# Recurrent outputs with tokens on partitions: scores and queries become the stationary operands, and reversed rows are shifted by DMA

## Chip, cores and metric

The kernel runs on one core of one Trainium2 chip. Times are device microseconds of one execution; the time of a kernel is the median of its runs. The engines are named as the profile names them: PE (matrix products), PEld (its weight loads), DVE (vector), ACT (scalar), POOL (GpSimd) and SP, whose queue issues all DMAs here.

## The reference

For 4 batches, 8 heads, 768 tokens and 40 features a head, a gated recurrence runs over the tokens; its output is laid out as rows of 320 features, mixed by a two-dimensional Fourier transform, normalised and passed through a two-layer network.

```python
for t in range(S):
    m_new = np.maximum(f_gate[:, :, t] + m, i_gate[:, :, t])
    f_stab = np.exp(f_gate[:, :, t] + m - m_new)
    i_stab = np.exp(i_gate[:, :, t] - m_new)
    C = f_stab * C + i_stab * outer(vt, kt)         # 40 x 40 a head
    n = f_stab * n + i_stab * kt
    h = C @ qt;  denom = np.maximum(np.abs(n . qt), 1.0)
    y[:, :, t] = sigmoid(o_gate[:, :, t]) * h / denom
x = y as (B, S, 320)
u = x + real(fft(fft(x, axis=1), axis=2))
un = (u - mean(u)) / sqrt(var(u) + 1e-6)
out = u + relu(un @ w_ch1) @ w_ch2                  # 320 -> 1280 -> 320
```

## The kernel before

**Tiles.** A chunk is 128 tokens, six to a batch. In batches 2 to 4 (numbered 1 to 3 in the code) a chunk is worked as two halves of 64 tokens, each with its own step of the state, and the 8 heads lie as two groups of four pairs (hip 0 and 1, pair p). Products on PE use a quarter of the array each (64 rows by 64 columns), and four of them, in the order TILES, run side by side. All values are fp32. What belongs to one chunk:

- `mlstm_load`, `mlstm_load_max`, `mlstm_load_decay` and `mlstm_load_o` fetch queries and keys (`qk`, features on partitions), keys and values with a column of ones (`kvt`, tokens on partitions), the running maxima (`W<-M_d`), the decays (`Gb<-G_d`) and the output gate (`so`). M_d and G_d are scratch in DRAM, written once in batch 1.
- `mlstm_exp` on ACT and `mlstm_mask` on POOL (L487) make the weights W of a pair of tokens; `halves_scores` makes the scores on PE, and `halves_weigh` on DVE (L643) multiplies them into W.
- `halves_to_state` makes the chunk's part of the next state on PE; `halves_decay` (POOL, L629) and `halves_add` (DVE, L638) build the state. Three state buffers rotate.
- `halves_from_state` multiplies the state (stationary) with the decayed queries qg (moving); `halves_from_chunk` multiplies the values (stationary) with W (moving), in two turns so that each turn's row groups write separate PSUM banks. A tiny ACT copy, `halves_between` (L670), stands between the turns. All small products are issued by the helper at L491. The result, `ph`, has features on partitions.
- `halves_gather` copies `ph` to SBUF on ACT (L568 to L579, with `mlstm_heads`), `halves_turn` transposes it on PE with four products against the identity (L681) so that tokens lie on partitions, and `mlstm_finish` on DVE (L696 to L703) divides by the denominator, applies the gate and writes rows of x. L703 is its last instruction and the last reader of the PSUM banks `heads`, in which both `ph` and the transposed copy lie.

**Order of tokens.** The Fourier part folds chunk c with chunk 5 - c, so chunks 2, 4 and 5 (BACKWARDS) hold their tokens in reverse and shifted by one; first tokens of chunks 0, 1 and 2 change places. `mlstm_heads` does this in its ACT copies; `h_first` is a small buffer on POOL for the swapped token.

**Order of work.** Every step is put into a plan by `at(slot, phase, function)`, and the plan is run in order of slot and phase (EVAC, FILL, MAIN, FILL_PE, that is 0 to 3). Engines execute their own instructions strictly in that order and wait for each other by semaphores. The network of one batch gives a slot its length (a block of products), and the recurrence of a later batch is filled in between: the recurrence of code batch 1 stands in slots 32 to 52, that of 2 from slot 50, that of 3 from 82, three slots a chunk. In `plan_halves`, with s the chunk's first slot, scores come at s, from_state and from_chunk at s+3, the copy at s+4, the transposes at slots s0 + (7, 10, 13, 16, 19, 19), the finish one slot after them.

Lines that also appear: L1013, L1022, L1084 and L1089 are products of the network's first layer, L1147 and L1203 of the second; L379 to L399 convert weights from float64 bits on DVE and ACT; L858 to L901 are products of the Fourier part, L944 its transposes; `mix_fold` (L778 to L797) adds and subtracts the chunk pairs of x, on DVE and partly POOL. L331 and L332 are transposes of weights that `halves_of_chunks` makes once for batches 2 to 4, and L335 and L336 their copies to SBUF.

Of the kernel before, what the change touches and what calls it, by code (L numbers as in the profile page):

```python
# [42 lines left out]
ORDER = (0, 5, 1, 4, 2, 3)  # L43
M_INIT = -1.0e30
# [8 lines left out]
def kernel(  # L53
# [87 lines left out]
    def gates(gp):  # L141
# [161 lines left out]

        def maxima_out():
            nc.sync.dma_start(out=M_d.rearrange("c i p t -> p c i t"), in_=M[0:BH].rearrange("p c (i t) -> p c i t", i=2))

        def halves_of_chunks(step):
# [8 lines left out]
            elif step == 1:  # L316
# [3 lines left out]
                nc.sync.dma_start(out=G_d[:, H:].rearrange("c p t -> p c t"), in_=g[H:BH])  # L320
            elif step == 2:
                d2 = late["dec2"] = free[0:BH, 3 * S:3 * S + BH // 2 * NS].rearrange("p (n c) -> p n c", c=NS)
                ends = g[0:BH].rearrange("p c (i t) -> p (c i) t", i=2)[:, :, LH - 1]
                nc.gpsimd.tensor_tensor(out=d2, in0=ends.unsqueeze(1).to_broadcast([BH, BH // 2, NS]),
                                        in1=spread_sb[:, L:].unsqueeze(2).to_broadcast([BH, BH // 2, NS]), op=OP.mult)
            elif step == 3:
                p2 = ps_h.tile([L, NT * BH + BH // 2 * NS], FP, name="p2", tag="ph")
                pt, pd = p2[:, 0:NT * BH], p2[:, NT * BH:]
                late["p2"] = [t.rearrange("p (n c) -> p n c", c=n) for t, n in ((pt, BH), (pd, NS))]
                for c in range(NT):  # L330
                    nc.tensor.transpose(late["p2"][0][:, c, :], wk[:, c, :], ident[0:BH, 0:BH])  # L331
                nc.tensor.matmul(late["p2"][1], spread_sb[:, 0:L], late["dec2"], start=True, stop=True)  # L332
            else:
                pt, pd = late["p2"]
                nc.vector.tensor_copy(out=colT[:, :, 1, H:], in_=pt[:, :, H:])  # L335
                nc.vector.tensor_copy(out=decB[:, NP:], in_=pd[:, NP:])  # L336

        at(12, FILL + 0.7, maxima_out)
        at(1, FILL + 0.2, parts, last)
# [9 lines left out]
        for n, (s, phase) in enumerate(((16, FILL + 0.2), (18, FILL + 0.3), (19, FILL + 0.4), (21, FILL_PE + 0.5),  # L349
                                        (26, FILL + 0.8))):  # L350
            at(s, phase, halves_of_chunks, n)
# [132 lines left out]
    def mlstm_mask(b, c):  # L484
        for i in range(2):
            W = chunks[b, c].W[i * LH:(i + 1) * LH]
            nc.gpsimd.affine_select(out=W, in_=W, compare_op=OP.is_ge, fill=0.0, base=0, pattern=[[0, H], [1, LH]],  # L487
                                    channel_multiplier=-1)
# [70 lines left out]
    def mlstm_heads(b, c, ph, parts=False):  # L559
# [3 lines left out]
        if b > 0:  # L563
            hT, before = (t.rearrange("p (hip m) t -> p hip m t", hip=2) for t in (hT, before))
        every, first, later = (tuple([slice(None)] * (len(ph.shape) - 1) + [t]) for t in
                               (slice(0, L), slice(0, 1), slice(1, L)))
# [27 lines left out]
    def side(n):  # L594
        return banks["heads"].rearrange("p hip (s m t) -> p s hip m t", s=2, t=L)[:, n]

    TILES = ((0, 0), (1, 1), (0, 1), (1, 0))

    def columns(c, n):

        return LH if c == 0 else n

    def halves_scores(b, c):
# [5 lines left out]
        for p in range(NP):  # L609
            for hip, i in TILES:  # L610
                r, t = slice(hip * 64, hip * 64 + D), slice(i * LH, (i + 1) * LH)
                product(k.ps[t, hip, p, :], k.qk[r, 1, p, t], k.qk[r, 0, p, t], True)

    def halves_to_state(b, c):
        k = chunks[b, c]
        for p in range(NP):
            for i, hip in TILES:
                if 2 * c + i < NS - 1:
                    r, h, n = slice(i * LH, (i + 1) * LH), hip * NP + p, columns(c, D)
                    product(k.pc[hip * 64:hip * 64 + n, i, p, :], k.k[r, h * D:h * D + n], k.vw[r, h, :], True)  # L620
# [11 lines left out]
    def halves_add(b, c, i):  # L632

        k, n = chunks[b, c], 2 * c + i
        if n == 0:
            nc.vector.tensor_copy(out=halves_state(k, 1), in_=k.pc[:, 0])
        elif n < NS - 1:
            nc.vector.tensor_tensor(out=halves_state(k, i + 1), in0=halves_state(k, i + 1), in1=k.pc[:, i], op=OP.add)  # L638
# [6 lines left out]
    def halves_from_state(b, c):  # L645

        k = chunks[b, c]
        k.ph = side(0)
        for m in range(2):
            for i in range(2):  # L650
                for hip, e in TILES:
                    if 2 * c + i > 0:
                        r, t, p = slice(hip * 64, hip * 64 + D), slice(i * LH, (i + 1) * LH), 2 * m + e
                        product(k.ph[e * 64:(e + 1) * 64, hip, m, t], k.C[i][r, p * D1:p * D1 + LH], k.qg[r, p, t],
                                m == 0 and i == (c == 0))

    def halves_from_chunk(b, c, turn):
# [4 lines left out]
        for m in range(2):  # L662
            for i, e in TILES:
                hip, n = i ^ turn, columns(c, D1)
                r, h = slice(i * LH, (i + 1) * LH), hip * NP + 2 * m + e
                product(k.ph[e * 64:e * 64 + n, hip, m, r], k.v[r, h * D1:h * D1 + n], k.W[r, h, :], False)

    def halves_between(b, c):

        nc.scalar.copy(out=warm[0:1, 0:1], in_=chunks[b, c].ph[0:1, 1, 1, L - 1:L])  # L670

    def halves_gather(b, c):
        k = chunks[b, c]
        k.hT = hT_bufs[(b * NT + c) % 2]
        mlstm_heads(b, c, k.ph)

    def halves_turn(b, c):
        k = chunks[b, c]
        px = side(0 if c == NT - 1 else 1)
        for p in range(NP):  # L680
            nc.tensor.transpose(px[:, p // 2, p % 2], k.hT[:, p, :], ident)  # L681
        k.px = px

    def mlstm_finish(b, c):

        k = chunks.pop((b, c))
        if c == 0:
            xs[b] = x_bufs[b % 2]
        px = k.px.rearrange("p (a pr) t -> p a pr t", a=2) if b == 0 else k.px
        h1 = px.rearrange("p a pr (two e) -> p a (pr two) e", two=2)  # L690
# [11 lines left out]
        x, sc = (t.rearrange("p (a h d) -> p a h d", a=2, d=D) for t in (xs[b][:, c, 0:DM], k.so))  # L702
        nc.vector.tensor_tensor(out=x, in0=h1[:, :, :, 0:D], in1=sc, op=OP.mult)  # L703

# [21 lines left out]
    def plan_halves(b, s0, stride=3):  # L726
        for c in range(NT):
            s = s0 + stride * c
            end = c == NT - 1
# [16 lines left out]
            at(s + 3, MAIN - 0.1 if end else FILL_PE, halves_from_state, b, c)  # L746
            at(s + 3, MAIN - 0.1 if end else FILL_PE, halves_from_chunk, b, c, 0)
            at(s + 3, MAIN if end else FILL_PE + 0.5, halves_between, b, c)
            at(s + 3, FILL_PE + 3, halves_from_chunk, b, c, 1)
            at(s + 4, FILL - 0.6, halves_gather, b, c)  # L750
            at(s + 4, FILL + 0.35, mlstm_tanh, b, c)
            t = s0 + (7, 10, 13, 16, 19, 19)[c]
            at(t, FILL_PE + 0.5, halves_turn, b, c)
            at(t + 1, MAIN + 0.55, mlstm_finish, b, c)
# [545 lines left out]
    plan_batch(2, 50, 83, s_mlp + 2 * MLP_SLOTS)  # L1300
    plan_batch(3, 82, 115, s_mlp + 3 * MLP_SLOTS)
# [102 lines left out]
def _layout(q, k, v, o_gate):  # L1404
# [4 lines left out]
    def token_major(t):  # L1409
        return t.reshape(B, H, NT, L, D).transpose(0, 2, 3, 1, 4)  # L1410

    qkT = np.stack([feature_major(q), feature_major(k)], axis=4)
# [3 lines left out]
    o = o_gate.transpose(0, 2, 1, 3).reshape(B, S, DM)[:, _tokens()]  # L1416
# [29 lines left out]
```

## Time and profile before

| | us |
|---|---|
| runs, median (lowest to highest) | 408.74 (404.95 to 409.12), 3 runs |
| profiled execution, its own time | 410.02 |
| its span, first to last instruction | 408.3 |
| busy: PE, PEld, DVE, ACT, POOL | 390.9, 285.3, 281.3, 182.1, 129.1 |

The chip's granted PE clock averages 0.99 of full speed in the profile. The recurrence of batches 2 to 4 lies between 62 and 284 us; from about 300 us on only the last batch's Fourier part and network remain. In a line of instructions the numbers are start and duration in us (timeline), or busy us, mean ns of one and idle time before them with what ended it (groups). A line of waits has who waited for whom, us in total, times, and the longest.

### The profile page before, as it was taken

What the parts mean: (1) busy time and instruction counts of PE and PEld (TensorE: products, weight loads), DVE (VectorE), ACT (ScalarE), POOL (GpSimd) and SP (SyncE); (2) the same over time, 40 slices, a digit from 0 to 9 for tenths busy, and PEclk for the clock granted to TensorE, in tenths of its full rate; (3) what the DMA queues carried; (4) which work ended last, traced back from release to release, by engine and by line L of the source; (5) the groups of instructions that cost most, each with busy time, mean ns of one, the idle gap of its engine ahead of it and who ended that gap; (6) DMA issues with size and microseconds to landing.
All of it is one profiled execution on the core that took longest, in us unless ns stands there. A gap on an engine that the chain in (4) does not pass through costs nothing.

```text
span 408.3 us, 10669 instructions
## 1 busy us (share of the span) xinstructions
PE 390.9 (96%) x4246; PEld 285.3 (70%) x4246; DVE 281.3 (69%) x669; ACT 182.1 (45%) x510; POOL 129.1 (32%) x228
## 2 busy tenths in 40 slices
PE   8999999999979999998999999998999999999996
PEld 6877555556547677765559998855569997556996
DVE  8789986798846539675874579966764786335652
ACT  6987258577640232555464315553450122455000
POOL 5555314477940641240074233440230000020000
PEclk9999999989999999999999999999999999999999
DMA  7989499487643352375001444300000000000000
GB/s 217 289 229 309 114 232 270 157 240 216 166 119 109 113 136 86 99 206 161 0 10 36 139 122 151 108 4 2 0 2 6 28 33 34 0 0 2 32 34 32
DMA packets 23836, 43.29 MB, mean 106 GB/s; under 512 B 5076, under 2 KB 12972, under 8 KB 23660
## 3 DMA queue, kind: packets, MB, share of 16 engines
q1 hardware_dynamic: 23788, 42.63, 35.8%
q8 instruction: 33, 0.54, 0.6%
q14 instruction: 15, 0.12, 0.1%
HBM read 38.49 MB, written 4.12 MB: 104 GB/s over the span
## 4 chain that ended last, share of the span: by engine, by line
PE 80%; DVE 12%; issue 3%; ACT 3%; POOL 1%; POOLq 0%; DVEq 0%; ACTq 0%
PE po L1203 17%; PE pm L1084 16%; PE po L1147 8%; PE pm L1089 5%; PE pm L1022 5%; PE ph L491 4%; PE ps L491 3%; PE pu L901 3%; PE pz L870 2%; PE ph L681 2%; PE put L944 1%; DVE stats L928 1%; PE pm L1013 1%; PE pz L858 1%; PE ph L532 1%
## 5 line engine op out<-in xcount | busy, mean ns | idle before, releaser
L1153 DVE SCALAR_TENSOR_TENSOR x<-po,rstd,x 128x160 f32<-128x160 f32 (+1 forms) x69 | 26.9, 394 | 38.0 <-PE po L1203 35.3
L1093 DVE TENSOR_TENSOR h<-h,pm 128x384 f32<-128x384 f32 x60 | 30.7, 550 | 31.2 <-PE pm L1084 17.2
L1084 PE MATMUL pm<-uT,w_sb 128*128 128x384 f32 x90 | 37.3, 501 | 0.2 <-DVE uT L1072 0.2
L464 ACT ACTIVATE W<-W,colT 128x64 f32<-128x64 f32 x144 | 37.4, 340 | 0.0
L1147 PE MATMUL po<-w_sb,h 128*128 128x320 f32 x120 | 36.1, 451 | 0.0
L629 POOL TENSOR_TENSOR C<-C,decB 128x164 f32<-128x164 f32 x30 | 17.3, 577 | 55.8 <-DVE C L638 45.5
L487 POOL TENSOR_SCALAR_AFFINE_SELECT W<-W 64x512 f32<-64x512 f32 x36 | 28.3, 785 | 17.2 <-ACT W L464 16.1
L1022 PE MATMUL pm<-uT,w_sb 128*128 128x384 f32 x80 | 31.4, 521 | 0.6 <-issue 0.4
L1147 PEld LDWEIGHTS po<-w_sb,h 128*128 128x128 f32 x120 | 23.0, 196 | 10.0 <-issue 1.6
L1203 PE MATMUL po<-T,S 128*128 128x160 f32 x180 | 28.0, 302 | 0.2 <-DVE x L1153 0.2
L474 POOL TENSOR_TENSOR qg<-qk,Gb 128x512 f32<-128x512 f32 (+1 forms) x21 | 27.2, 1297 | 1.1 <-DMA Gb<-G_d 1.1
L1203 PEld LDWEIGHTS po<-T,S 128*128 128x128 f32 x180 | 25.4, 190 | 1.8 <-DVE x L1153 0.5
L1203 PE MATMUL po<-w_sb,h 128*128 128x160 f32 x180 | 26.4, 301 | 0.0
L1203 PEld LDWEIGHTS po<-w_sb,h 128*128 128x128 f32 x180 | 25.1, 190 | 1.2 <-DVE x L1153 0.3
L1089 PE MATMUL pm<-uT,w1t_sb 64*128 64x384 f32 x120 | 25.4, 510 | 0.0
L670 ACT COPY warm<-ph 1x1 f32<-1x1 f32 x18 | 2.6, 147 | 48.6 <-PE ph L491 44.9
L1084 PEld LDWEIGHTS pm<-uT,w_sb 128*128 128x128 f32 x90 | 15.5, 189 | 12.5 <-DVE h L1093 3.6
L1140 ACT ACTIVATE h<-h 128x384 f32<-128x384 f32 x45 | 23.1, 520 | 2.0 <-DVE h L1093 2.0
L968 POOL TENSOR_TENSOR t<-rstd 128x6 f32<-128x6 f32 x12 | 3.1, 256 | 65.3 <-DVE v L962 64.8
L949 ACT COPY uT<-put 128x384 f32<-128x384 f32 x24 | 11.1, 476 | 26.4 <-PE put L944 26.4
L480 POOL TENSOR_TENSOR vw<-kvt,colT 128x328 f32<-128x328 f32 x23 | 18.2, 792 | 13.6 <-DVE colT L335 11.0
L1022 PEld LDWEIGHTS pm<-uT,w_sb 128*128 128x128 f32 x80 | 14.7, 201 | 10.0 <-issue 3.4
(233 smaller groups left out, 879.8 us busy)
## 6 DMA issues: line engine op xcount, KB each, us to landing
kvt<-in_kv SPq DMA_DIRECT2D x24, 336.0 KB
qk<-in_qkT SPq DMA_DIRECT2D x48, 160.0 KB
raw<-in_w SPq DMA_DIRECT2D x10, 640.0 KB
Gb<-G_d SPq DMA_DIRECT2D x36, 128.0 KB
W<-M_d SPq DMA_DIRECT2D x36, 128.0 KB
so<-in_o SPq DMA_DIRECT2D x24, 160.0 KB
out<-x SPq DMA_DIRECT2D x24, 160.0 KB
ds_sb<-in_dft_s SPq DMA_DIRECT2D x1, 1155.0 KB
```

The source lines that it names most:

```text
L464: nc.scalar.activation(out=k.W[:, h, :], in_=M, func=AF.Exp, scale=-1.0, bias=colT[:, c, 0, b * H + h:b * H + h + 1])
L474: nc.gpsimd.tensor_tensor(out=k.qg[:, :, t], in0=k.qk[:, 0, :, t], in1=k.Gb[:, :, t], op=OP.mult)
L487: nc.gpsimd.affine_select(out=W, in_=W, compare_op=OP.is_ge, fill=0.0, base=0, pattern=[[0, H], [1, LH]], channel_multiplier=-1)
L491: nc.tensor.matmul(out, w, x, start=start, stop=True, skip_group_check=True)
L1022: nc.tensor.matmul(k.pm[i], w1_sb[:, ch, f0:f0 + L], u[2 * ch], start=(ch == 0 and not ahead), stop=(ch == 1 and ahead), skip_group_check= ...
L1084: nc.tensor.matmul(bank, w, u, start=start, stop=True, skip_group_check=True)
L1089: nc.tensor.matmul(bank, block(w1t_sb, i)[rows], mlp_u(gr, 1)[rows], start=False, stop=True, skip_group_check=True)
L1093: nc.vector.tensor_tensor(out=h, in0=h, in1=bank, op=OP.add)
L1140: nc.scalar.activation(out=h, in_=h, func=AF.Relu, scale=-1.0)
L1147: nc.tensor.matmul(k.po, hidden(gr, f)[:, i * L:(i + 1) * L], w2_sb[:, f, :], start=(f == 0), stop=(f == NFF - 1))
L1153: nc.vector.scalar_tensor_tensor(out=u, in0=po, scalar=k.rstd[:, c:c + 1], in1=u, op0=OP.mult, op1=OP.add)
L1203: nc.tensor.matmul(po, a[:, f], w[:, f], start=start and f == 0, stop=f == half - 1, skip_group_check=True)
```

## The change

The recurrent outputs of batches 2 to 4 are made with tokens on the output's partitions at once. In from_state, qg is now stationary and the state moves; in from_chunk, W is stationary and the values move. So `ph` comes out as rows of tokens and `mlstm_finish` reads it straight from PSUM: `halves_gather`, `mlstm_heads` and `halves_turn` are no longer used in these batches.

[...] So in odd pairs the two token halves are swapped on partitions in keys, values, maxima, weights and column factors (`kv` on the host, `other_halves`, `maxima_out`, step 4 of `halves_of_chunks`); `halves_add` collects its two banks accordingly.

The reversal of chunks 2, 4 and 5 goes into the data: queries and output gates are reversed on the host, maxima and decays on POOL before they go to DRAM. What remains is a shift by one row, and `halves_rows` does it with DMAs from `so`, to which `mlstm_finish` now writes in those chunks. The plan changes: finish at s+4, rows at s+5, no special place for the last chunk, step 3 of `halves_of_chunks` in slot 24 instead of 21, and the recurrences of batches 3 and 4 one slot later.

```diff
+RUNS = ((0, 2, False), (2, 3, True), (3, 4, False), (4, 6, True))
+        def other_halves():
+            odd = [colT[i * LH:(i + 1) * LH, :, 0, H + 1:BH:2] for i in range(2)]
+            kept = gp.tile([LH, NT, (BH - H) // 2], FP, name="kept")
+            for out, in_ in ((kept, odd[0]), (odd[0], odd[1]), (odd[1], kept)):
+                nc.gpsimd.tensor_copy(out=out, in_=in_)
         def maxima_out():
-            nc.sync.dma_start(out=M_d.rearrange("c i p t -> p c i t"), in_=M[0:BH].rearrange("p c (i t) -> p c i t", i=2))
+            m, in_ = (t.rearrange("p (n t) -> p n t", t=LH) for t in (free[0:BH, 0:S], flat(M, slice(0, NT))))
+            for c0, c1, back in RUNS:
+                n = slice(2 * c0, 2 * c1)
+                nc.gpsimd.tensor_copy(out=m[:, n], in_=backwards(in_[:, n], LH - 1, LH) if back else in_[:, n])
+            m = m.rearrange("p (c i) t -> p c i t", i=2)
+            for odd in range(2):
+                for i in range(2):
+                    nc.sync.dma_start(out=M_d[:, i ^ odd, odd:BH:2].rearrange("c p t -> p c t"), in_=m[odd:BH:2, :, i])
...
-                nc.sync.dma_start(out=G_d[:, H:].rearrange("c p t -> p c t"), in_=g[H:BH])
+                for c0, c1, back in RUNS:
+                    v = g[0:BH, c0:c1]
+                    if back:
...
+                        nc.gpsimd.tensor_copy(out=v, in_=backwards(g[0:BH, c0:c1], L - 1, L))
+                    nc.sync.dma_start(out=G_d[c0:c1, H:].rearrange("c p t -> p c t"), in_=v[H:BH])
...
-                nc.vector.tensor_copy(out=colT[:, :, 1, H:], in_=pt[:, :, H:])
+                nc.vector.tensor_copy(out=colT[:, :, 1, H:BH:2], in_=pt[:, :, H:BH:2])
+                for i in range(2):
+                    nc.vector.tensor_copy(out=colT[i * LH:(i + 1) * LH, :, 1, H + 1:BH:2],
+                                          in_=pt[(1 - i) * LH:(2 - i) * LH, :, H + 1:BH:2])
...
+        at(13, FILL + 0.7, other_halves)
-        ... (21, FILL_PE + 0.5)      # step 3 of halves_of_chunks
+        ... (24, FILL_PE + 5.4)
...
     def halves_from_state(b, c):
-        k.ph = side(0)
-        for m in range(2):
-            for i in range(2):
-                for hip, e in TILES:
-                    if 2 * c + i > 0:
-                        r, t, p = slice(hip * 64, hip * 64 + D), slice(i * LH, (i + 1) * LH), 2 * m + e
-                        product(k.ph[e * 64:(e + 1) * 64, hip, m, t], k.C[i][r, p * D1:p * D1 + LH], k.qg[r, p, t],
-                                m == 0 and i == (c == 0))
+        k.ph = banks["heads"][:, :, 0:NP * D1].rearrange("p hip (m d) -> p hip m d", d=D1)
+        for p in range(NP):
+            for hip, i in TILES:
+                if 2 * c + i > 0:
+                    r = slice(hip * 64, hip * 64 + D)
+                    t = queries(c, i)
+                    product(k.ph[t, hip, p, :], k.qg[r, p, t], k.C[i][r, p * D1:(p + 1) * D1], p == 0)
     def halves_from_chunk(b, c, turn):
         for m in range(2):
-            for i, e in TILES:
-                hip, n = i ^ turn, columns(c, D1)
-                r, h = slice(i * LH, (i + 1) * LH), hip * NP + 2 * m + e
-                product(k.ph[e * 64:e * 64 + n, hip, m, r], k.v[r, h * D1:h * D1 + n], k.W[r, h, :], False)
+            for j, i in TILES:
+                p, hip = 2 * m + (i ^ j), j ^ turn
+                h = hip * NP + p
+                product(k.ph[queries(c, i), hip, p, :], k.W[rows(j), h, :], k.v[rows(j), h * D1:(h + 1) * D1],
+                        2 * c + i == 0 and m == turn == 0)
-    def halves_gather(b, c): ...
-    def halves_turn(b, c): ...
...
+    def halves_rows(b, c):
+        x, y = xs[b][:, :, 0:DM], chunks[b, c].x
+        def move(out, in_):
+            nc.sync.dma_start(out=out, in_=in_)
+        if c == 2:
+            move(x[0:1, 2], x[0:1, 0])
+            move(x[0:1, 0], x[0:1, 1])
+        if c in BACKWARDS:
+            move(x[1:L, c], y[0:L - 1])
+            move(x[0:1, 1 if c == 2 else c], y[L - 1:L])
...
-            at(s + 3, MAIN - 0.1 if end else FILL_PE, halves_from_state, b, c)
-            at(s + 3, MAIN - 0.1 if end else FILL_PE, halves_from_chunk, b, c, 0)
-            at(s + 3, MAIN if end else FILL_PE + 0.5, halves_between, b, c)
+            at(s + 3, FILL_PE, halves_from_state, b, c)
+            at(s + 3, FILL_PE, halves_from_chunk, b, c, 0)
+            at(s + 3, FILL_PE + 0.5, halves_between, b, c)
             at(s + 3, FILL_PE + 3, halves_from_chunk, b, c, 1)
-            at(s + 4, FILL - 0.6, halves_gather, b, c)
             at(s + 4, FILL + 0.35, mlstm_tanh, b, c)
-            t = s0 + (7, 10, 13, 16, 19, 19)[c]
-            at(t, FILL_PE + 0.5, halves_turn, b, c)
-            at(t + 1, MAIN + 0.55, mlstm_finish, b, c)
+            at(s + 4, MAIN + 0.55, mlstm_finish, b, c)
+            at(s + 5, FILL - 0.6, halves_rows, b, c)
...
-    plan_batch(2, 50, 83, s_mlp + 2 * MLP_SLOTS)
-    plan_batch(3, 82, 115, s_mlp + 3 * MLP_SLOTS)
+    plan_batch(2, 51, 83, s_mlp + 2 * MLP_SLOTS)
+    plan_batch(3, 83, 115, s_mlp + 3 * MLP_SLOTS)
```

## The prediction, made before the changed kernel was run

> **What bounds the kernel now.** Batches go by the code's numbers, 0 to 3; the change is to 1, 2 and 3. I read the page first, then the groups by shape on the tensor engine (PE), then the waits on PE, then stretches of the timeline.
>
> ```profile
> PE 390.9 (96%) x4246; PEld 285.3 (70%) x4246; DVE 281.3 (69%) x669; ACT 182.1 (45%) x510; POOL 129.1 (32%) x228
> ...
> PE 80%; DVE 12%; issue 3%; ACT 3%; POOL 1%; POOLq 0%; DVEq 0%; ACTq 0%
> ```
>
> PE is busy for 96% of the span and carries 80% of the chain that ended last. So an instruction taken off PE is worth its full slot on PE, wherever PE doesn't then wait. The exceptions are the waits on PE; their view has few lines that matter:
>
> ```profile
> PE ph L491 <- DVE x L703: 4.3, 6, 1.3
> PE ps L491 <- issue: 2.1, 1, 2.1
> ...
> PE ph L491 <- ACT warm L670: 0.7, 1, 0.7
> PE ph L491 <- DVE W L643: 0.5, 1, 0.5
> ```
>
> The largest belongs to the part that is changed: six times PE stands at halves_from_state until the last instruction of mlstm_finish (L703) on DVE is done, because that one still reads the PSUM banks of `heads`. The groups by shape give the PE work concerned, all batches together (one fp32 product shows as two records, a transpose as one):
>
> ```profile
> L491 PE MATMUL ph<-W,kvt 64*41 64x64 f32 x480 | 13.0, 217 | 1.3 <-ACT warm L670 0.7 <-DVE W L643 0.5
> ...
> L491 PE MATMUL ph<-qg,C 40*64 40x64 f32 x528 | 11.9, 225 | 4.5 <-DVE x L703 4.3 <-POOL W L487 0.2
> L681 PE MATMUL ph<-ident,h 128*128 128x128 f32 x72 | 10.5, 275 | 0.0
> ```
>
> The means are latencies; four small tiles run side by side, so price is read from starts.
>
> [...] The trace agrees that stationary columns count: in the timeline of the weight loads, to_state has 41 moving columns both times, once with 64 stationary columns (chunk 0) and once with 40:
>
> ```profile
> 214.78 0.56 PEld L491 LDWEIGHTS ps<-qk 40*64 40x64 f32 x32 [0.55 <-issue]
> 215.24 0.56 PEld L491 LDWEIGHTS ps<-vw,kvt 64*64 64x64 f32 x32
> ...
> 227.36 0.56 PEld L491 LDWEIGHTS ps<-qk 40*64 40x64 f32 x32
> 227.83 0.43 PEld L491 LDWEIGHTS ps<-vw,kvt 64*40 64x40 f32 x32
> ```
>
> 64 stationary by 41 moving takes 0.56 us for 32 records, exactly as 64 by 64; only 40 by 41 is shorter. From the starts, groups of four come every 58 ns and 41 ns. [...] Here L1022 runs at half pace (640 ns a record instead of some 330) just after PE had lost 1.3 us at 80 to 82 us, and L1147 after the 2.1 us of "issue" at 117[...]. [...]
>
> **The change part by part**, against the profiled execution (410.0 us; 408.3 of span; the median of the runs shown is 408.7).
>
> 1. Transposes (halves_turn) go. Four per chunk, 18 chunks. Next to other work:
>
> ```profile
> 264.73 1.56 PE L1084 MATMUL pm<-uT,w_sb 128*128 128x384 f32 x4
> 266.12 0.60 PE L681 MATMUL ph<-ident,h 128*128 128x128 f32 x4
> 266.56 0.81 PE L1084 MATMUL pm<-uT,w_sb 128*128 128x384 f32 x2
> ```
>
> From 266.12 to 266.56: 0.44 us of PE per chunk, all on the path: 18 x 0.44 = -7.9 us.
>
> 2. Products. from_state turns from (64 stationary, 64 moving) into (64, 41), from_chunk from (41, 64) into (64, 41). By the loads above each group of four stays at 58 ns: 0. If moving columns did count, 276 groups (1104 records) would each gain 17 ns: -4.7. I take 0 and keep -4.7 for the range; the reverse, a loss, is excluded by the 64 by 41 row.
>
> 3. The wait on L703. Before, finish(c) comes in the plan one slot or less ahead of the from_state that it blocks (for the last chunk from_state is moved to the front of its slot):
>
> ```profile
> 185.18 0.60 PE L681 MATMUL ph<-ident,h 128*128 128x128 f32 x4
> ...
> 187.05 0.49 DVE L703 TENSOR_TENSOR x<-ph,so 128x320 f32<-128x320 f32 x1
> 187.69 0.51 PE L491 MATMUL ph<-qg,C 40*64 40x64 f32 x19 [1.26 <-DVE x L703]
> ```
>
> After, finish(c) stands at slot s+4 and the next from_state at s+6, about 1.5 slots later, a slot being 1.7 to 2.8 us. Moving batches 2 and 3 one slot later puts their finishes into the same slots as the old finish of the chunk before, so DVE gets there at old times: for batch 2 at 158.6, 172.0, 181.8 and 187.5, where the new from_state (the old start plus one slot, less the stalls and transposes saved) falls near 162, 175, 183.6 and 189.4, an estimate. Margins of 1.8 us or more: the waits of batches 2 and 3 go, and the one at 113 us is replaced (see 4): -4.3.
>
> 4. Batch 1, where DVE is saturated with weight conversion. There DVE runs two slots behind PE, and finish(0) now stands between L381 and L643 in DVE's order:
>
> ```profile
> 79.40 0.69 PE L491 MATMUL ph<-qg,C 40*64 40x64 f32 x32
> ...
> 79.49 0.48 DVE L381 TENSOR_SCALAR m<-raw 128x640 uint32<-128x640 uint32 x1
> ...
> 79.89 0.68 DVE L643 TENSOR_TENSOR W<-ps,W 128x512 f32<-128x512 f32 x1
> ...
> 80.63 0.44 PE L491 MATMUL ph<-W,kvt 64*41 64x64 f32 x16 [0.54 <-DVE W L643]
> ...
> 82.62 0.43 PE L491 MATMUL ph<-W,kvt 64*41 64x64 f32 x16 [0.75 <-ACT warm L670]
> ```
>
> A finish is 0.17 + 0.17 + 0.20 + 0.5 + 0.5 = 1.6 us. So from_state(1) waits from 79.4 to 81.5. The old waits of 0.54 and 0.75 lie behind it and are mostly absorbed (W would be ready at 82.2, the second turn at 83.1 against 82.6): +0.5. What is queued behind finish(0) on DVE is L643, L638 and a conversion; nobody needs the conversions before 119 us. The other finishes of batch 1 end an estimated 1.5 to 3 us ahead of their from_state, except finish(4), which with DVE 1.6 to 3 us later than before ends near 112 against PE at 111.8: +0.5.
>
> 5. ACT loses the copies of heads (18 of 0.58, and small ones), POOL the h_first copies that waited for them. Neither is on PE's path; 0, a help to 4.
>
> 6. The new row moves on SP: 2 DMAs for chunks 4 and 5, 4 for chunk 2, 24 in all. [...] Chunk 2's moves overwrite what the one before reads[...]; behind it wait decay loads due four slots later and the next chunk's. The fold that needs rows of chunk 5 comes two slots or more after; cover is 4 us at least. 0; without cover +2 per batch. x rows are also still being stored by the batch before: finish(1) of batch 3 shares its slot with the store of the same row, but L700 (1.28 us there) runs meanwhile. For this and DVE's heavier 236 to 251 us I take +0.5, from 0 to +3.
>
> 7. Early part. POOL gets 4 copies before the M_d DMA (an estimated 1.5 us from its 0.32 us for 161 columns), in a stretch where it is idle for 2.4 us; the table loads issue some 1.5 us later than their 31.6, with their first product at 43.5. The G_d reversals put 0.7 us ahead of the fold on POOL, used at once: +0.3. The seven small PE products of step 3 leave the chain at 47.95 (0.9 us up to 48.85) for a stretch where PE idles: -0.9. Two more DVE copies: +0.3. Together -0.3, from -1 to +2.
>
> Sum: -7.9 + 0 - 4.3 + 0.5 + 0.5 + 0.5 - 0.3 = -11.0. Against 410.0 that is 399.0, against the median 397.7; I say 398.
>
> **The rivals.**
>
> A (forecast, 0.55): transposes and waits go, products keep their pace: 398; own range 394.5 to 401.5.
>
> B (0.12): moving columns count as well, the -4.7 of step 2: 393. For it: 40 by 41 is faster than 64 by 64. Against: the 64 by 41 row.
>
> C (0.20): DVE takes PE's place as the bound from 75 to 113 and 236 to 251 us, where it is at 26 of 30 us, and half of the waits return: 402 to 405, say 403.
>
> D (0.13), slower. `ph` now has one copy in PSUM, read by DVE itself, where ACT used to free it. If DVE lags PE by more than 1.5 slots at most joints of chunks, each of the 15 from_states after a chunk waits as in step 4: 2.1 us[...]. It decides from four joints on: -11 + 4 x 3.8 = +4, so 413 (over 1% slower); six give 420. For it: the lag at 79 us. Against: DVE's own idle stretches, 46 us from 140 to 300 us.
>
> **How the numbers follow.** A measurement of this kernel can tell about 1%, that is 4.1 us. Faster by over 1% (below 404.6) are A, B and most of C: 0.82; within 1%: the rest of C and the weak end of D: 0.07; slower: 0.11. The range goes from B's 392.5 to C's 405, leaving out D and a little of A and B. [...]
>
> **What would show it.** Right: no L681; the line of waits on L703 (its new number) reduced to batch 1; 32 records of ph still 0.56 us of weight loads; ACT some 13 us less busy; the L1203 stretches after 300 us the same length. Wrong: PE waits on finish in batches 2 and 3 (C, D), weight loads of ph at 0.43 (B), DVE's fold waiting for a DMA (step 6), or PE busy falling by less than 7 us.

## The result, and the profile after

Batches go by the code's numbers, 0 to 3, as in the prediction. The changed kernel takes 434.41 us (median of 4 runs, 431.03 to 436.71) against 407.78 for the kernel before on the same chip: 1.0656 times as long, with a 95% interval from 1.0561 to 1.0752. The forecast was 398.0 us and a range up to 405.0; neither its direction nor its range held.

The page of the kernel after (span 435.0 us), with PE's busy time, the granted clock in 40 slices, and the chain that ended last by engine and by line:

```profile
PE 395.3 (91%) x4174; PEld 285.1 (66%) x4174; DVE 281.1 (65%) x671; ACT 172.3 (40%) x480; POOL 132.2 (30%) x231
...
PEclk9999999899898899968959999999989999999999
...
PE 52%; DVE 22%; DMA 17%; issue 3%; ACT 2%; POOL 2%; SPq 1%; DVEq 0%; POOLq 0%; ACTq 0%
PE po L1235 17%; PE pm L1116 12%; DMA x<-so 9%; PE po L1179 5%; PE pm L1121 4%; PE pu L933 3%; DMA out<-x 2%; DMA Gb<-G_d 2%; PE ph L519 2%; DMA spread_sb<-in_spread 2%; DVE so L719 2%; PE ps L519 2%; PE pz L890 1%; PE pz L902 1%; DMA raw<-in_w 1%
```

The 72 records of the transposes are gone (4246 to 4174), yet PE is busy for longer, at a lower share, with a clock that falls to 5 and 6 tenths in places. And an entry that the chain of before did not have, the row move `x<-so`, holds 9% of it. The waits name who stands for it (line, engine and tile, then us in total, times, longest); first those of DVE and PE, then those of SP's queue:

```profile
DVE eo L810 <- DMA x<-so: 19.8, 4, 8.5
...
PE pm L1121 <- DVE h L1125: 8.3, 2, 5.8
...
PE pz L902 <- DVE fe L817: 6.1, 3, 5.3
...
PE po L1235 <- DVE x L1185: 5.1, 3, 2.7
DVE x L723 <- DMA out<-x: 5.0, 2, 2.6
```

```profile
SPq L731 <- DVE so L723: 33.9, 5, 15.4
...
SPq L478 <- DMA x<-so: 15.7, 3, 5.3
...
SPq L466 <- DMA x<-so: 5.3, 1, 5.3
```

L810 is the fold of two chunks of x: four times it stands for a row move, and what PE needs from DVE stands behind it. SP, whose queue is served in order, stands behind the same moves with the loads of decays (L478) and maxima (L466) of later chunks. (The first line of SP is SP standing for finish before it may issue a move; the version of 112 + 15 rows below has 30.3 us of it too, and costs nothing that can be told from having no moves.) One such joint, batch 2's last fold, in the timelines of DVE, PE and SP (start, length, and in brackets the idle time before and who ended it):

```profile
209.63 1.48 DVE L1125 TENSOR_TENSOR h<-h,pm 128x384 f32<-128x384 f32 x3
217.50 0.49 DVE L810 TENSOR_TENSOR eo<-x 128x320 f32<-128x320 f32 x1 [6.39 <-DMA x<-so]
```

```profile
214.95 0.91 PE L1121 MATMUL pm<-uT,w1t_sb 64*128 64x384 f32 x2
221.62 2.92 PE L1121 MATMUL pm<-uT,w1t_sb 64*128 64x384 f32 x6 [5.77 <-DVE h L1125]
```

```profile
206.60 2.11 SPq L731 DMA_DIRECT2D x<-so  x2
208.75 0.89 SPq L454 DMA_DIRECT2D qk<-in_qkT  x2
209.68 0.41 SPq L456 DMA_DIRECT2D kvt<-in_kv  x1
210.21 1.12 SPq L466 DMA_DIRECT2D W<-M_d  x2
211.42 0.62 SPq L478 DMA_DIRECT2D Gb<-G_d  x1
```

DVE is free for the fold at 211.11 and gets its rows 6.39 us later; the adds of the network's first layer stand behind the fold in DVE's order, so PE stops for 5.77 us. The move was issued at 206.60. Its 127 packets of 1280 bytes start one after another, the first at 207.87, the last ending at 216.70. After the decay load at 211.42 SP's next DMA, a second decay load that takes nothing from the move, is issued only at 217.19. It is the eighth after the move: in the trace the 246 DMAs of SP signal eight semaphores in turn (numbers 101 and 104 to 110, each back at the eighth DMA after), and the load of 217.19 waits for 105, which is the move's, before it takes it. The same holds for all four waits of L478 and L466 above (5.34, 5.31, 5.30 and 5.15 us, behind the moves with 107, 104, 106 and 105). The DMA view of the move before it (199.2 to 206.7 us, queue: packets, MB, share of 16 engines) shows how few engines work on it:

```profile
q1 hardware_dynamic: 160, 0.16, 6.7%
```

6.7% of sixteen engines is 1.07 engines: the move ran in single file. The prediction priced such a move without asking how many engines would carry it.

PE's idle stretches of 5.25, 3.56 and 5.77 us in the changed kernel cost twice, for half clock began within each (at 137.54, 188.74 and 219.46 us). Mean granted clock and PE's busy time in two pairs of slices (us, PE, PEld, DVE, ACT, POOL busy, PEclk, DMA share, GB/s), around the fold of batch 1 and that of batch 2:

```profile
130.00:140.00 10.00, 4.75 (x124) 3.48 (x122) 1.51 (x5) 1.36 (x7) 2.82 (x3) 0.88 0.50 126
140.00:150.00 10.00, 10.00 (x28) 6.32 (x28) 5.91 (x14) 2.75 (x10) 4.56 (x6) 0.78 0.65 180
215.00:225.00 10.00, 4.23 (x10) 1.91 (x10) 5.98 (x16) 0.90 (x2) 3.37 (x13) 0.72 0.61 149
225.00:235.00 10.00, 10.00 (x32) 5.59 (x31) 4.01 (x8) 5.37 (x15) 3.35 (x7) 0.77 0.43 126
```

The stretch after each gap has PE busy all the time at a mean clock of 0.77 or 0.78. Behind these means stand two levels: the granted clock is 0.50 from 137.5 to 144.4 us and from 219.5 to 229.7, and 1.00 after each. Up to its last microseconds the changed kernel has 37.5 us at half clock. The kernel before has 6.8, from 83.11 to 86.52 and from 120.66 to 124.07, with PE busy all the time: two stretches of 3.41 us, each worth an estimated 1.7 us (half its length). Not every gap is followed by such a stretch: one comes after 1.49 us of idle time at 82 us in the changed kernel, none after the 2.72 us that end there at 261.74, and none after 1.50 us at 82 in the 112 + 15 version below. Nor does it take a long gap: in the kernel before, gaps of 0.54 and 0.75 us stand ahead of the half clock that begins at 83.11, and one of 2.09 us ahead of the other. What brings it on was not shown.

### The profile page after: what moved, and what is told of

Read it like the earlier page. It is cut to its first block, busy times and chain, and to the rows that moved or that the text cites. A ratio compares the mean times of both kernels' runs of the same rounds, so it can differ in the third digit from the quotient of the medians.

```text
span 435.0 us, 10563 instructions
## 1 busy us (share of the span) xinstructions
PE 395.3 (91%) x4174; PEld 285.1 (66%) x4174; DVE 281.1 (65%) x671; ACT 172.3 (40%) x480; POOL 132.2 (30%) x231
## 4 chain that ended last, share of the span: by engine, by line
PE 52%; DVE 22%; DMA 17%; issue 3%; ACT 2%; POOL 2%; SPq 1%; DVEq 0%; POOLq 0%; ACTq 0%
PE po L1235 17%; PE pm L1116 12%; DMA x<-so 9%; PE po L1179 5%; PE pm L1121 4%; PE pu L933 3%; DMA out<-x 2%; DMA Gb<-G_d 2%; PE ph L519 2%; DMA spread_sb<-in_spread 2%; DVE so L719 2%; PE ps L519 2%; PE pz L890 1%; PE pz L902 1%; DMA raw<-in_w 1%
## 5 line engine op out<-in xcount | busy, mean ns | idle before, releaser
L1116 PE MATMUL pm<-uT,w_sb 128*128 128x384 f32 x90 | 41.8, 554 | 6.1 <-DVE h L1125 5.6
L1179 PE MATMUL po<-w_sb,h 128*128 128x320 f32 x120 | 37.2, 464 | 0.0
L1121 PE MATMUL pm<-uT,w1t_sb 64*128 64x384 f32 x120 | 26.6, 529 | 8.3 <-DVE h L1125 8.3
L1116 PEld LDWEIGHTS pm<-uT,w_sb 128*128 128x128 f32 x90 | 17.3, 211 | 21.6 <-DVE h L1125 11.6
L1179 PEld LDWEIGHTS po<-w_sb,h 128*128 128x128 f32 x120 | 24.2, 206 | 11.1 <-issue 3.2
L501 POOL TENSOR_TENSOR qg<-qk,Gb 128x512 f32<-128x512 f32 (+1 forms) x21 | 28.2, 1343 | 8.6 <-DMA Gb<-G_d 8.5
L1054 PE MATMUL pm<-uT,w_sb 128*128 128x384 f32 x80 | 29.5, 506 | 0.1
L1121 PEld LDWEIGHTS pm<-uT,w1t_sb 64*128 64x128 f32 x120 | 12.8, 192 | 20.6 <-DVE h L1125 9.6
L1235 PEld LDWEIGHTS po<-w_sb,h 128*128 128x128 f32 x180 | 25.2, 190 | 1.4 <-DVE x L1185 0.3
L1134 ACT COPY h<-pm 128x384 f32<-128x384 f32 x15 | 7.2, 477 | 37.0 <-PE pm L1116 37.0
```

Source lines behind the costliest of these rows:

```text
L501: nc.gpsimd.tensor_tensor(out=k.qg[:, :, t], in0=k.qk[:, 0, :, t], in1=k.Gb[:, :, t], op=OP.mult)
L1054: nc.tensor.matmul(k.pm[i], w1_sb[:, ch, f0:f0 + L], u[2 * ch], start=(ch == 0 and not ahead), stop=(ch == 1 and ahead), skip_group_check= ...
L1116: nc.tensor.matmul(bank, w, u, start=start, stop=True, skip_group_check=True)
L1121: nc.tensor.matmul(bank, block(w1t_sb, i)[rows], mlp_u(gr, 1)[rows], start=False, stop=True, skip_group_check=True)
L1179: nc.tensor.matmul(k.po, hidden(gr, f)[:, i * L:(i + 1) * L], w2_sb[:, f, :], start=(f == 0), stop=(f == NFF - 1))
L1235: nc.tensor.matmul(po, a[:, f], w[:, f], start=start and f == 0, stop=f == half - 1, skip_group_check=True)
```

## The experiments

All rest on the changed kernel unless said otherwise. Each ratio is against the kernel before, run on the same chip. The theories: T1, the shape of the move of 127 rows; T2, the number of row DMAs and SP's order, whatever their shape; T3, the moved finish.

**112 + 15 rows instead of 127.**

```
-            move(x[1:L, c], y[0:L - 1])
+            move(x[1:113, c], y[0:112])
+            move(x[113:L, c], y[112:L - 1])
```

> The move of 127 rows is cut in two, 112 rows and 15 rows; the values are the same. Theory T1 (the shape: a move of 127 rows has its packets one after another, 7 to 9 us, where a load of 128 rows has them side by side): the 112 rows land within 3 us, the fold's waits for row moves fall from 19.8 us to 3 or less, and the time falls from 434 to 402-412 us. Theory T2 (the number of row DMAs on SP's queue, each waiting its turn, whatever the shape): one DMA more for each of the nine chunks, so 434 to 438. Theory T3 (the moved finish: VectorE's order and its waits for the stores): the moves don't matter, 430 to 436.

Measured: 404.08 us, ratio 0.9952 (0.9930 to 0.9974). T1's prediction, by one DMA more per chunk, which T2 says must not help. The first move of 112 rows is issued at 99.37 and has its packets from 101.28 to 102.10, so it lands in 2.7 us; the 15 rows run side by side within 0.3 us. The DMA view from 101.25 to 102.10:

```profile
q1 hardware_dynamic: 128, 0.14, 57.6%
```

Nine of sixteen engines on average, against 1.07. The fold's waits for row moves are gone from the list of waits. PE is busy 381.6 us instead of 395.3, and PE's gaps of more than 0.1 us (added up from its timeline, from 30 us on) are 14.7 us instead of 33.6. So of the 32.9 us between the two spans, 19 were standing still and 13.7 were the same 4174 records taking longer: half clock for 37.5 us in the one profile, for 3.4 in the other.

**128 rows instead of 127**, unshifted:

```
-            move(x[1:L, c], y[0:L - 1])
+            move(x[0:L, c], y[0:L])
```

> The move has 128 rows instead of 127, unshifted (so the rows of chunks 2, 4 and 5 are not where they should be); number, order and place of the DMAs are unchanged. T1: the 128 packets lie side by side and land within 2.5 us, time 402 to 412 us. T2: 432 to 436, as with 127 rows. T3: 430 to 436.

Measured: 404.25 us, ratio 0.9947 (0.9925 to 0.9968). One row more, with the same number, order and place of DMAs, takes away 30 us: the first move's 128 packets run from 101.96 to 102.56. It is the count and not the shift by a row, for the 112 + 15 rows are shifted too. T2 and T3 as main causes have fallen.

**No row moves at all** (finish writes x for every chunk, `halves_rows` is not planned):

> All row moves of batches 1 to 3 are left out (chunks 2, 4 and 5 keep the rows that the products gave them, so those outputs have other rows), finish writes x for every chunk. This is the whole price of the moves. T1 and T2 both say 398 to 406 us (what is left are the waits for stores, 3 to 5 us of TensorE idle, against the 398.0 predicted without them). T3 says 420 us or more.

Measured: 403.67 us, ratio 0.9959 (0.9934 to 0.9984). Moves that are spread over the engines cost 0.4 us by the two medians (404.08 and 403.67), which is less than can be told apart: the prediction's zero for them held, once they land fast. It also says that part of the forecast is missing for another reason: 6 us against the 398.0, and as a change on the same chip more, for the 112 + 15 version gains 2.7 us (406.73 less 404.08) of the 11.0.

**The moves issued, but into a tile that nobody reads:**

```
-        k.x = k.so if b > 0 and c in BACKWARDS else xs[b][:, c, 0:DM]
+        k.x = xs[b][:, c, 0:DM]
...
-            move(x[1:L, c], y[0:L - 1])
+            move(side[1:L], y[0:L - 1])
```

> The same row moves are issued at the same place, with the same sizes, but into the output-gate tile of the chunk, which nobody reads afterwards; finish writes x for every chunk and the fold reads that at once (rows of chunks 2, 4 and 5 not shifted). It parts the two ways in which a slow move costs: the fold that waits for it, and SP's queue that stands behind it and issues later loads late. If the fold's wait is most of it (T1a): 408 to 418 us. If the late loads behind SP are most of it (T1b, T2): 425 to 434. T3: 430 or more.

Measured: 415.97 us, ratio 1.0298 (1.0218 to 1.0378). Without the fold's wait 18.4 us come back; the other 11.9 us (415.97 less 404.08) stay, and are paid by what comes behind the moves, as the waits of SP and DVE show. (By the three ratios the two parts are nearer to equal, some 14 us each.)

```profile
SPq L478 <- DMA so<-x: 15.6, 3, 5.4
```

```profile
DVE x L723 <- DMA out<-x: 12.3, 3, 5.2
```

Not only loads are late here: stores stand behind the moves, and finish waits for them before it may write the rows (2.2 us in the kernel without moves). And SP's order is not the only way: in the changed kernel a gate load issued at 104.67, while a move ran, has the last eight of its 128 packets from 111.88 to 112.30, after the move's last at 111.19. So this load was not complete before the move was, though its other packets lie between 106.1 and 107.4. In this kernel finish writes x in chunks 2, 4 and 5 too, where the changed one leaves that wait to SP, so the split between the two ways is rough.

**Other row counts**, chunk 2 as 126 + 1, chunk 4 as 120 + 7, chunk 5 as 96 + 31:

> The 127 rows are cut in three ways: chunk 2 as 126 + 1, chunk 4 as 120 + 7, chunk 5 as 96 + 31. If a move is spread only where its rows are a multiple of 16 (or fewer than 16): 126 and 120 rows run one after another, 7 to 9 us, 31 rows about 2 us, and the time is 420 to 432 us. [...] only 31 rows run in single file for about 2 us, and the time is 403 to 408 us.

Measured: 405.23 us, ratio 0.9980 (0.9949 to 1.0011). By the packet records 126 rows take 0.9 us (101.74 to 102.64), but 31 rows run in single file from 190.71 to 193.06. So it is not a multiple of 16 that counts. The two counts that ran in single file, 127 and 31, are primes; what decides it beyond the counts tried was not shown. From 101.7 to 102.65 us, while the 126 rows move, the engines are busy for 57.3%, or 9.2 of sixteen on average, 44 small packets of other DMAs among the 170. The DMA view of a stretch in the middle of the 31 rows (191.2 to 191.8):

```profile
q1 hardware_dynamic: 10, 0.01, 6.6%
```

**Where the rest of the forecast is.** In the 112 + 15 version no product of batches 2 and 3 waits for finish for more than 0.3 us any more. But PE now has gaps that the kernel before did not have, in the network's layers:

```profile
233.22 1.69 PE L1236 MATMUL po<-T,S 128*128 128x160 f32 x10 [2.72 <-DVE x L1186]
...
249.13 1.63 PE L1236 MATMUL po<-T,S 128*128 128x160 f32 x10 [2.35 <-DVE x L1186]
```

Between two residuals (L1186) DVE works off, before the first gap, two adds of 1.65 us each, finish with 1.6, the masking product with 0.68 and a state add with 0.31. Before the second, finish stands for a store:

```profile
245.99 0.49 DVE L723 TENSOR_TENSOR x<-ph,so 128x320 f32<-128x320 f32 x1 [2.87 <-DMA out<-x]
```

Six kernels tried to move that by the order of work, all built on the 112 + 15 version.

Finish and moves one slot later in batches 2 and 3 (s+5 for s+4):

> The 112 + 15 version with finish and the row moves one slot later in batches 2 and 3 (finish no longer lies in a slot with the next chunk's masking by VectorE, and stands behind the residuals of that slot and further from the previous batch's stores). If the rest of the missed gain is VectorE's order around finish (rival C of the prediction): the TensorE gaps of 2.72 us at 233 and 2.35 us at 249 and the wait of 2.9 us for a store go, and the time is 398 to 401 us against 404. If those gaps only move elsewhere (VectorE is short of time there whatever the order): 403 to 406.

Measured: 405.93 us, ratio 0.9963 (0.9934 to 0.9992). The second expectation: the gap at the residual falls to 1.10 us, and the products wait for finish instead, four times by 0.78 to 1.52 us after 230 us.

The same, and in batch 1 finish and the masking product ahead of the slot's weight conversions:

> As the run before, and in batch 1 finish and the masking product on VectorE stand ahead of that slot's weight conversions. If the TensorE gaps of 1.50 us at 82 and 0.88 us at 98 are the conversions ahead of finish (step 4 of the prediction): 1.5 to 2.5 us less than the run before, 396 to 399. If the conversions are late next and the weights wait: no gain, 398 to 401.

Measured: 409.09 us, ratio 1.0037 (1.0010 to 1.0064): worse, a miss. The gap of 1.50 us at 82 goes, but PE now waits 1.41 us at 82.78 for a state add (L670) and 1.34 us at 85.13. The two edits were not taken apart.

Batches 2 and 3 one slot earlier again (slots 50 and 82). In this kernel the second finish of batch 3 stands ahead of batch 1's last residual to the same rows, so those outputs have other values:

> The 112 + 15 version with batches 2 and 3 started one slot earlier again, as in the kernel before (slots 50 and 82). It undoes the one-slot shift of the change. If the shift placed finish badly against the adds and the residuals: 400 to 402 us. If it placed it well: 405 to 408. If the shift is worth nothing: 403 to 405.

Measured: 407.43 us, ratio 1.0016 (0.9986 to 1.0046). The shift by a slot is needed for the result's meaning, and by the two ratios it is worth 0.6%, some 2.6 us.

Batch 3 one slot later still (84):

> The 112 + 15 version with batch 3 started one slot later (84 for 83), so that its first finish stands a slot behind the two adds of batch 2 and its second no longer shares a slot with the store that it waits for. If the gaps of 2.72 us at 233 and 2.35 us at 249 come from that meeting (rival C, and the store): both fall under 1 us and the time is 400 to 402 us against 404. If VectorE is short of time there wherever finish lies: 403 to 406, with the gaps at other instructions.

Measured: 405.43 us, ratio 0.9976 (0.9945 to 1.0007). The gaps at the residuals fall to 1.83 and 1.51 us, but one of 2.48 us appears at 260, where the sums for the next network (L1105) come late. Again moved, not removed.

One of the two adds of the first slot moved a slot on (`(4, 5, 5, 6, 8, 9)` for `(4, 4, 5, 6, 8, 9)` in `plan_batch`):

> The 112 + 15 version with the second of the two adds of batches 2 and 3's first slot (chunk 5) moved one slot later; nothing else. The residual that TensorE waits for at 233 us then has 1.7 us less of VectorE's work ahead of it. If it is the sum of adds and finish ahead of the residual: the gap of 2.72 us falls to about 1, the time by 1 to 2 us, 402 to 403. If finish alone makes it: no change, 404.

Measured: 403.21 us, ratio 0.9905 (0.9868 to 0.9942); the first gap falls to 1.08 us, about 1 as expected, and the second stays (2.67 us). Both changes of order together (finish later, ahead of the adds, adds spread):

> The 112 + 15 version with both: finish and the moves one slot later in batches 2 and 3, finish ahead of that slot's adds, and the adds spread. If the order on VectorE is what is left of the missed gain: the gaps over 0.3 us behind finish, residuals and stores after 150 us sum to under 3 us (8.3 us in the 112 + 15 version), and the time is 397 to 401 us. If VectorE's time itself is short there: 402 to 405.

Measured: 404.93 us, ratio 0.9955 (0.9923 to 0.9987): no gain over the spread alone; the products wait for finish again, 1.52 us at 180 and at 270.

**A second copy of the sums in PSUM**, used in turn by chunk, so that the next products need no finish:

```
+        at_ = 256 * (c % 2)
-        k.ph = banks["heads"][:, :, 0:NP * D1]...
+        k.ph = banks["heads"][:, :, at_:at_ + NP * D1]...
```

> The spread version (112 + 15 rows, adds spread) with two copies of the products' sums in their PSUM banks, used in turn by chunk, finish where the change put it. The next chunk's products then need no finish. If the single copy is what turns a late finish into TensorE's wait: the gaps of 1.50 us at 82 and 0.89 at 98 go (or become waits for W, at most half as long) and nothing changes after 150 us, where TensorE waits for residuals: 401 to 402.5 us against 403.2. If the single copy costs nothing: 403 to 404.

Measured: 404.27 us, ratio 0.9939 (0.9903 to 0.9975); the gaps at 82 and 98 did not go. With finish one slot later:

> As e14, and finish and the moves one slot later in batches 2 and 3. With one copy that only changed which instruction of TensorE waited (405.9 against 404.1). If the short window between products, finish and the next products is the rest of the missed gain: the gaps behind finish, residuals and stores after 150 us sum to under 3 us and the time is 397 to 400 us. If VectorE's time there is short whatever the window: 402 to 405.

Measured: 407.25 us, ratio 1.0034 (1.0003 to 1.0064). Two slots later:

> As e14, with finish and the moves two slots later in batches 2 and 3, about where the kernel before has its finish. Same two theories: short window 396 to 400 us; VectorE short of time 402 to 405. If it is worse than e15 by over 1 us, the fold of those batches has become late.

Measured: 443.24 us, ratio 1.0928 (1.0872 to 1.0984), with waits of PE that no copy had taken away, and 37.5 us at half clock. The late fold of the expectation is not among PE's waits:

```profile
PE ph L519 <- DVE x L724: 14.8, 6, 5.0
PE ph L519 <- DVE so L724: 13.4, 4, 4.3
```

And with finish reading each head half on its own:

> As e15 (two copies, finish one slot later in batches 2 and 3), and finish reads each head half of the sums in an instruction of its own, so that no read spans the bank of the other half (three instructions more on VectorE for each chunk, about 0.6 us). In e15 the products still waited for finish of the chunk before, 1.50 us at 82 and 8 us after 150 us. If that wait came from reads that span both banks: it goes, and the window theory is tried at last: 397 to 401 us if the short window is the rest of the missed gain, 402 to 405 if VectorE's time is. If the wait stays (products and finish in one bank wait for one another): 405 to 409, as e15 and a little more.

Measured: 409.49 us, ratio 1.0051 (1.0018 to 1.0084):

```profile
240.63 0.68 PE L519 MATMUL ph<-C,qg 40*64 40x41 f32 x32 [2.89 <-DVE x L728]
```

The products wait for finish in another part of the same bank. The last edit did not part the halves: the first product starts at 240.63, after the read of the second half ended at 240.49. Whether the bank or the whole tile, in which both banks and both copies lie, is what ties products and reads together, the four runs do not tell: a copy in another bank or tile was not tried, and so neither was a longer window. The runs do show what a late finish costs: 28 us of waits at two slots. That is the mechanism of rival D, though not in the kernel as changed.

**VectorE's time itself.** The spread version without mean and variance of the adds in batches 2 and 3:

```
+        if b > 1:
+            return
         stats = st_p.tile([L, 6], FP, name="stats", tag="stats")
```

> The spread version (e10) without the mean and variance of the adds of batches 2 and 3 (0.67 us of VectorE's time for each of the 12 adds; those batches are then normalised with older numbers); nothing else. If VectorE's time ahead of the residuals is the rest of the missed gain: the gaps of 1.08 us at 231, 2.67 at 246 and 1.00 at 320 lose 0.7 us or more each, and the time is 400 to 401.5 us against 403.2. If not: 403 to 404, the gaps as they were (what sets them is then finish, or its wait for the store).

Measured: 398.84 us (4 runs), ratio 0.9786 (0.9715 to 0.9857): with 5.7 us less of DVE's busy time (279.3 to 273.6) the median is 4.4 us lower, more than expected. Not all of it is the edit's: of the 3.4 us of gaps that are gone, 1.1 lie before 150 us, where the edit changes nothing. The gap at 231 falls from 1.08 to 0.36 us and one of 1.00 at 320 goes; the one at 246 hardly changes:

```profile
230.27 1.63 PE L1238 MATMUL po<-T,S 128*128 128x160 f32 x10 [0.36 <-DVE x L1188]
244.44 1.63 PE L1238 MATMUL po<-T,S 128*128 128x160 f32 x10 [2.23 <-DVE x L1188]
```

So DVE's time is what is short at the first, and the store's wait is left as the candidate for the second. The last run takes the store's wait away:

```
-        k.x = k.so if b > 0 and c in BACKWARDS else xs[b][:, c, 0:DM]
+        k.x = k.so if b > 0 and c in BACKWARDS or (b, c) == (3, 1) else xs[b][:, c, 0:DM]
...
+        if (b, c) == (3, 1):
+            move(x[:, 1], y)
```

> The spread version (e10), in which the second chunk's finish of batch 3 no longer writes into the rows that the store of batch 1 still reads: its result stays in the output-gate tile and a DMA of 128 rows carries it to x behind that store, as for chunks 2, 4 and 5. If VectorE's wait for the store makes the gap of 2.67 us at 246: the gap falls under 0.7 us and the time by 1.5 to 2.5 us, to 400.5-402 against 403.2. If VectorE's own work makes it: 403 to 404.

Measured: 399.69 us (399.08 to 400.37, 6 runs), ratio 0.9818 (0.9772 to 0.9864). The gap that was 2.67 us at 246 is 0.46 us, so the store had made it:

```profile
231.91 1.63 PE L1238 MATMUL po<-T,S 128*128 128x160 f32 x10 [1.08 <-DVE x L1188]
...
244.31 1.62 PE L1238 MATMUL po<-T,S 128*128 128x160 f32 x10 [0.46 <-DVE x L1188]
```

This version, with 112 + 15 rows, one add a slot later and one finish behind its store by way of a DMA, beats both kernels: 1.8% under the kernel before, and by the two medians 8% under the changed one.

The sums, in us (span and busy from the pages, gaps of PE over 0.1 us from its timeline):

| kernel | span | PE busy | PE gaps |
|---|---|---|---|
| before | 408.3 | 390.9 | 11.7 |
| after | 435.0 | 395.3 | 33.6 |
| 112 + 15 rows | 402.1 | 381.6 | 14.7 |
| and add spread | 399.6 | 379.9 | 13.8 |
| and finish off the store | 398.0 | 380.3 | 11.9 |

## Why the prediction was wrong, step by step

**Step 6, the row moves, is the step that failed.** Its term was +0.5, from 0 to +3; it measured 30.3 us (434.41 less 404.08; 28.7 by the two ratios). The landing was put short, by an estimate of the author's that no row of the trace before showed. It measured 8.8 us of packets, 10.1 from issue to last packet at the joint of batch 2. The cover was right: from issue to the moment when DVE could fold, 211.11 less 206.60 is 4.5 us, and the step said 4 at least. But a cover of 4 us is nothing against 10. "Without cover +2 per batch" was too small as well: it left out that DVE's fold is in front of the adds that PE needs at once, that idle of 5.77 us came with 10.2 us at half clock, and that the loads and stores behind a slow move are late too (12 to 14 us of the 30). The step counted each queue that the moves stand in, but with the short landing.

**Step 1, transposes, -7.9.** They are gone. PE's busy time falls by 9.3 us in the 112 + 15 version. The 1.4 us beyond the forecast are about what the clock gave: the profile before has 6.8 us at half clock with PE busy, this one 3.4, and half of the difference, an estimated 1.7 us, is what that was worth.

**Step 2, products, 0.** Held. Weight loads of the turned products, after:

```profile
202.37 0.56 PEld L519 LDWEIGHTS ph<-C,qg 40*64 40x64 f32 x32 [0.55 <-issue]
202.83 0.33 PEld L519 LDWEIGHTS ph<-kvt,W 64*64 64x64 f32 x16
```

32 records take 0.56 us as before. Rival B falls with that.

**Step 3, the wait on finish, -4.3.** Half right. For batches 2 and 3 the products' wait is gone in the 112 + 15 version. But the step looked only at who waits for finish, not at whom finish now stands in front of: 2.72 and 2.35 us of waits at residuals, and twice 1.04 us at the adds of the first layer, where finish and the next chunk's masking product share a slot. That is rival C's mechanism, VectorE short of time, at one of the two places which it named (236 to 251 us), though it is not the waits on finish that return. The 404 of the 112 + 15 version lies near C's 403 in part by luck: as a change on the same chip it is 2.7 us, where C has about 6. Part of it was not DVE's time but a store, which step 6 had seen and taken for hidden.

**Step 4, batch 1, +0.5 twice.** The wait came as forecast, 1.49 us at 81.93 in the changed kernel. At 114.79 us the changed kernel starts after 1.89 us of waiting for finish(4), because the load of its output gate was late behind a move (112.30, as told above); with 112 + 15 rows that is gone, and 0.88 us at 98 came instead.

**Step 5** held, though ACT loses 9.8 us of busy time (182.1 to 172.3) where some 13 were expected. **Step 7**, -0.3: the first scores of batch 1 start 0.6 us later than before (62.64 for 62.04), inside its bounds.

**Rival D** forecast a slower kernel, but by waits on finish in batches 2 and 3. The changed kernel waits for finish only twice, both times in batch 1 (1.49 and 1.89 us), so D's direction came out right by luck. Its 3.8 us a joint were the 2.1 us of step 4 and an estimate of 1.7 for half clock behind every such wait. In the changed kernel 3.41 us at half clock did come behind either wait, from 82.93 and from 117.06 us, but none behind the 1.50 us of the 112 + 15 version.

With the row count mended and two places on DVE reordered, the profiles differ by 10.3 us (408.3 to 398.0), where the sum was -11.0. That flatters the sum: the profile before is longer than each of the three runs beside it (410.02 against at most 409.12), with 6.8 us at half clock and the stall of 2.1 us. The last version's profile has neither. The runs on one chip give 7.2 us (406.85 to 399.69).

## What to carry to other kernels

Before a DMA is costed, see in a trace whether a move with its row count goes side by side: 127 rows went in single file in 8.8 us, 126 of the same length in 0.9, and 112 + 15 cost nothing that could be measured. A slow DMA on a queue that also issues loads and stores is paid twice here, by who needs its data and by what comes behind it. And when an instruction is moved earlier to end a wait, ask of the slot where it arrives whose work it now precedes: here finish freed the products and held up the residuals.

## What the runs showed of the hardware that was not expected

A move between two tiles of SBUF whose 127 rows are 1280 bytes each ran one packet at a time, mostly 55 ns each, 58 to 148 ns under other traffic and up to 338 ns in single cases; 128 such rows went side by side within 0.6 us. A load of 128 rows issued at 104.67 us, while a move ran, got its last eight packets from 111.88 us, only behind the move's last at 111.19. And 31 rows took 2.35 us, more than twice the 126 rows.

Two copies in one PSUM bank were no double buffer here: in four kernels the matmuls into one part of the bank still waited for VectorE's reads of the other, up to 5.0 us at a time. Whether that goes by the bank or by the whole tile was not tried.
